# Alpha, k and q of the first six chunks: loaded four tokens per partition and turned by identity products

## The chip, the cores and the metric

The kernel runs on one NeuronCore of a Trainium2 chip. Its engines run side by side, each with its own queue of instructions that it takes in order: TensorE (PE) multiplies matrices and writes to PSUM, VectorE (DVE) and ScalarE (ACT) do element-wise work, GpSimd (POOL) does element-wise work on SBUF alone, and SyncE (SP) issues DMAs. PE loads the stationary operand of a product in a separate step, which the profile shows as PEld. The metric is the device time of one execution in microseconds (us).

## The reference

```python
# q, k, v, alpha: (4 batches, 8 heads, 768 tokens, 48), float32
for t in range(S):
    state = alpha[:, :, t, :, None] * state + np.einsum('bhd,bhe->bhde', k[:, :, t], v[:, :, t])
    y[:, :, t] = np.einsum('bhd,bhde->bhe', q[:, :, t], state)
x = y.transpose(0, 2, 1, 3).reshape(3072, 384)
h = x @ w_in                              # (384, 2048), float64
g = h * np.clip(h + 3.0, 0.0, 6.0) / 6.0
return (g @ w_out).astype(np.float32)     # (2048, 384), float64
```

A gated linear attention, which is a recurrence over the tokens, is followed by a feed-forward block with a hardswish gate. The weights go in as the bits of float64 and are turned into float32 on the chip.

## The kernel before

The recurrence is worked in chunks of 128 tokens: 24 chunks, six to a batch, in order. For each chunk the kernel loads alpha, k, q and v of all 8 heads (192 KB each), brings alpha, k and q into a layout with the head dimension on the partitions (two heads to a tile of 128 rows, 64 rows each, of which 48 are used) and the tokens on the free axis, takes the running products of alpha by two scans on DVE, scales k and q by them, and forms scores, attention and the new state on PE. Two chunks make a group of 256 tokens for the feed-forward block. Groups 0 and 1 are computed directly (`ff1`, `ff2`); from group 2 on the two products are split in the manner of fast matrix multiplication (`product1` with 20 products, `product` with 7), for which DVE adds up combinations of weights and activations.

Chunks 0 to 5 (`FIRST = 6`) come in by one way, and the later ones by another. For the first six, `load_akq` writes a ring tile with one token per partition and 8 heads of 64 places, 48 of them filled: runs of 48 numbers, 192 B each. `transposed` then turns it with four transposes on PE, one for each pair of heads, into a PSUM bank. Alpha is copied from there by ACT (`place_alpha`), k and q are read from PSUM by DVE (`scaled`). The 16 unfilled places are set once at the start, to 1 for alpha and 0 for k and q. From chunk 6 on, each partition takes four tokens, and DVE turns 32x32 blocks (`by_blocks`); no PE work is in that.

All work is issued in one order that is written out by hand as a string of steps (`run`), from which each engine gets its own instructions in that order. The steps that matter here, with a chunk as their first number:

- `la`, `lk`, `lq`, `lv`: loads of alpha, k, q, v; `w.i`: load of slice i of the weights (768 KB), all on SP's queue
- `ta`, `tk`, `tq`: turning alpha, k, q (L284; the second number is the PSUM bank); `ca`: alpha's copy on ACT (L302)
- `r`, `p`: the two scans on DVE (L311 with L315, L322); `k`, `q`: scaling (L334)
- `kb`: k back to tokens on the partitions, four transposes (L393); `ck`: its copy on ACT
- `sc`: scores (L365); `m`: mask (L375); `ya`, `yb`: attention (L478); `u`: update of the state (L452); `sm`, `st`, `sv`: the state's sums and copies (L462, L428, L438); `qa`: q for the second half of the chunk (L385); `cy`: the result to the feed-forward block (L487)
- `d1`, `d2`, `dx`, `d3`, `d4`: float64 bits of a slice to float32 (ACT L186, L196, L191, DVE L203 to L210, POOL L217)
- `fa`, `fb`, `f`: first product of groups 0 and 1 (L512, L501), `fr` and `fg` its gate (L517, L521); `b`: second product (L539)
- `x`, `y`, `xc`, `s`: sums of weights and activations on DVE; `M`, `n`, `o`: first product's pieces (L623, L629, L564 and around); `P`, `K`, `G`: second product's pieces (L726, L705, L742); `O`: store
- `z.0.n`: n products of the identity with itself into an unused bank (L555), fillers that keep PE running while it has nothing else to do

The order in which the string has them is thus the order on each queue, and a step that waits holds up what stands behind it on its engine.

Of the kernel before, what the change touches and what calls it, by code (L numbers as in the profile page):

```python
# [17 lines left out]
def kernel(  # L18
# [32 lines left out]
    nc = tc.nc  # L51
    B, H, S, D = q.shape
# [4 lines left out]
    NP = H // 2  # L57
# [3 lines left out]
    G = 2  # L61
# [11 lines left out]
    ident = consts.tile([C, C], FP, tag="ident")  # L73
# [10 lines left out]
    NR = 3  # L84
    NV = 3
    ring = {}
    rings = consts.tile([C, 3 * NR, H, 64], FP, tag="rings")
    for r in range(NR):
        for name, pad in (("a", 1.0), ("k", 0.0), ("q", 0.0)):
            t = ring[name, r] = rings[:, 3 * r + "akq".index(name)]  # L90
            (nc.vector if r == 0 else nc.gpsimd).memset(t[:, :, D:64], pad)

    vs, As = [], []
    for r in range(NV):
        t = consts.tile([C, 2, H, 64], FP, tag=f"v{r}", name=f"v{r}")
# [10 lines left out]
    for r in range(2):  # L106
        t = consts.tile([C, NP * W + 1], FP, tag=f"ax{r}")
        nc.vector.memset(t, 0.0)
        aX.append(t)
        t = consts.tile([C, NP * W], FP, tag=f"ini{r}")  # L110
# [7 lines left out]
    st, half_st, sm = (consts.tile([C, NP, D], FP, tag=name, name=name)  # L118
                       for name in ("st", "s1", "sm"))
# [115 lines left out]
    V = C // BLK  # L235
# [3 lines left out]
    for r in range(NQ):  # L239
        for name in "akq":  # L240
            quads[name, r] = consts.tile([C, NP, V, D], FP, tag=f"{name}q{r}",
                                         name=f"{name}q{r}")
# [5 lines left out]
    def pad(r):  # L248
        for name in "akq":
            for o in (BLK, 3 * BLK):  # L250
                nc.gpsimd.memset(quads[name, r][o : o + BLK, :, V - 1, D - BLK : BLK], 1.0)

    def load_akq(name, j):
        src = rows({"a": alpha, "k": k, "q": q}[name], j)
        if j < FIRST:
            nc.sync.dma_start(out=ring[name, j % NR][:, :, 0:D],
                              in_=src.rearrange("h s d -> s h d"))
            return
        to = quads[name, j % NQ]
        to = to.rearrange("r p v d -> r p (v d)")  # L260
        t = src.rearrange("(p a) (u v) d -> a u p (v d)", a=2, v=V)
        for o in range(4):
            skip = BLK * (o % 2)
            nc.sync.dma_start(out=to[BLK * o : BLK * (o + 1), :, 0 : V * D - skip],
                              in_=t[o // 2, :, :, skip : V * D])
# [10 lines left out]
    def transposed(name, j, i=None):  # L276
        if j >= FIRST:
            t = (K_t if name == "k" else Q_t)[j] = (Ks if name == "k" else Qs)[j % 2]
            by_blocks(t, name, j)
            return  # L280
        t = bank("t" + name, j, i)
        src = ring[name, j % NR]
        for p in range(NP):
            nc.tensor.transpose(  # L284
                t[:, p], src[:, 2 * p : 2 * p + 2].rearrange("s h d -> s (h d)"), ident)

    def by_blocks(to, name, j):
        nc.vector.transpose(out=to.rearrange("r p (u v) -> r p v u", v=V),
# [306 lines left out]
    for i in range(8):  # L595
        r, o = divmod(i, 3)
        spots.append(raws[r].rearrange("p n w -> p (n w)").bitcast(FP)[:, o * QB : (o + 1) * QB])
    xc = consts.tile([C, len(X_SUMS), C], FP, tag="xc")
# [68 lines left out]
    t = {1: b[0, 1], 2: spare[:, 0], 3: spare[:, 1], 4: spare[:, 2]}  # L667
# [100 lines left out]
    def run(words):  # L768
        for word in words.split():
            name, *at = word.split(".")  # L770
            steps[name](*(int(x) for x in at))

    with tc.manual_schedule():
        run("""z.0.5 z.0.3 z.0.1 qa.0.0 w.0 d2.0 d3.0 la.0 ta.0.0 z.0.8 lk.0 tk.0.1 la.1 ta.1.2
               lq.0 tq.0.3 lk.1 lv.0.0 d1.0 ca.0 r.0 p.0 k.0 kb.0.0 z.0.2 z.0.2 q.0 la.2 dx.0 ca.1
               r.1 ck.0 u.0.2.1 sm.0.0 qa.0.1 sv.0.1 tk.1.0 p.1 sc.0.2.3 w.2 lq.1 sm.0.1 k.1 m.0
               ta.2.0 z.0.2 d1.2 ca.2 d2.2 kb.1.0 ck.1 r.2 tq.1.2 q.1 dx.2 lv.1.1 u.1.3.1 z.0.3
               lq.2 w.1 lk.2 d4.0 lk.3 la.3 la.4 w.3 lq.3 lv.2.2 lk.4 w.5 pd.0 sv.0.0 pd.1 st.1
               sm.1.0 p.2 d3.2 sm.1.1 ya.0.3 yb.0 sc.1.0.2 m.1 d4.2 sv.1.1 cy.0 qa.1.1 sv.1.0 d1.1
               st.2 d2.1 dx.1 fa.0.1 tq.2.1 q.2 tk.2.3 k.2 fa.2.0 sc.2.0.2 d3.1 m.2 d4.1 ta.3.1  # L780
               ta.4.3 kb.2.0 qa.1.0 ca.3 r.3 ca.4 r.4 ya.1.2 yb.1 tk.3.1 fa.1.2 p.3 k.3 qa.2.1
               qa.2.0 cy.1 d2.3 d3.3 fb.2 fb.1 tq.3.1 q.3 sv.2.0 d1.3 ck.2 u.2.3.2 sm.2.0 d4.3
               fr.0.2.0 tk.4.0 d2.5 sv.2.1 k.4 sm.2.1 st.3 fg.0.2 d3.5 w.6 lv.3.0 lq.4 w.7 fb.0
               sc.3.1.3 m.3 kb.3.2 kb.4.0 f.0.3.3 ya.2.1 ck.3 d1.5 d4.5 d1.6 d2.6 d3.6 d4.6 sv.3.0
               qa.3.1 fr.0.1.0 fr.0.3.1 la.5 yb.2 u.3.3.2 sm.3.0 fg.0.3 fg.0.1 sm.3.1 f.0.5.0
               tq.4.3 f.0.6.3 ta.5.2 cy.2 ck.4 d2.7 qa.3.0 d1.7 d3.7 d4.7 fr.0.5.1 fr.0.0.0 sv.3.1
               fg.0.0 fg.0.5 p.4 ya.3.0 yb.3 f.0.7.2 qa.6.0 qa.12.0 qa.18.0 lq.7 w.4 d2.4 cy.3
               fr.0.6.1 w.9 d2.9 ca.5 d1.9 d1.4 dx.4 la.6 w.8 d3.4 lk.5 w.10 d3.9 ca.6 q.4 fg.0.6
               d4.9 w.12 d2.8 st.4 f.1.1.1 f.1.7.0 sc.4.0.2 f.1.3.3 qa.4.0 d1.8 fr.0.7.0 r.6 d3.8
               d4.8 d4.4 fg.0.7 m.4 fr.1.1.0 fr.1.7.1 fg.1.7 fg.1.1 d2.10 d1.10 f.1.0.2 d2.12 d3.10  # L790
               r.5 d4.10 fr.1.0.0 fr.1.3.1 fg.1.3 fg.1.0 d3.12 f.1.6.0 f.1.2.1 la.8 lq.5 lv.4.1
               w.11 w.13 lq.6 u.4.1.0 tk.5.3 sm.4.0 sv.4.0 d1.12 qa.4.1 d4.12 fa.4.3 fr.1.2.0
               fr.1.6.1 d2.11 d2.13 f.1.4.2 d1.11 sm.4.1 fg.1.2 k.5 kb.5.1 tq.5.3 d3.11 p.5 d4.11
               tq.6 fg.1.6 q.5 p.6 d3.13 d1.13 st.5 la.7 w.15 lv.5.0 lk.6 w.14 ck.5 b.0.0.1 fb.4
               ya.4.2 qa.5.1 sv.4.1 yb.4 sc.5.0.3 fr.1.4.1 cy.4 u.5.2 b.0.1 f.1.5.0 fr.0.4.0 d1.15
               sv.5.0 qa.5.0 lv.12.1 lk.7 lv.6.2 sv.12.0 sv.6.0 d4.13 xc.2.0 fg.1.4 q.6 xc.2.2
               sm.5.0 fg.0.4 ca.7 tk.6 sv.5.1 d2.15 d2.14 d1.14 d3.15 fr.1.5.1 d3.14 k.6 d4.14
               d4.15 fg.1.5 m.5 b.0.2 b.1.0.2 b.1.1 kb.6.0 ya.5.3 yb.5 b.1.2 cy.5 P.1.0.0 P.1.1.3
               lq.8 K.1.0 ck.6 u.6.2.3 b.1.3 bo.1 b.0.3 tq.7 y.5 y.1 y.3 y.0 y.6 x.0 y.9 y.7 xc.2.1
               y.11 y.13 y.2 y.8 xc.2.3 x.1 s.1.0.0 s.1.1.1 x.2 tk.7 y.10 s.1.2.3 G.1.0.0 y.4  # L800
               sm.6.0 P.1.3.3 xc.2.4 s.1.3.2 P.1.2 sc.6.2.1 y.16 y.12 y.15 s.1.4 r.7 y.17 y.19
               xc.2.5 y.20 s.1.5 xc.2.7 y.14 y.18 y.21 xc.2.6 y.23 lq.9 so.1 lv.7.0 lk.9 bo.0 K.1.2
               K.1.1 P.1.4 M.2.0.1 P.1.5 n.2.0.8 M.2.1 n.2.1.9 G.1.1.1 M.2.7.2 n.2.7.11 sv.6.1
               sm.6.1 k.7 G.1.2.2 xc.2.10 x.3 xc.2.8 p.7 q.7 st.7 y.22 xc.2.9 m.6 M.2.15.3 M.2.2
               n.2.2.10 M.2.8 kb.7.0 M.2.3 M.2.4 P.1.6 qa.7.0 ck.7 n.2.4.12 G.1.3.3 O.1.0 la.9 lk.8
               ca.9 o.2.0.0 M.2.9 u.7.1.2 ya.6.0 e.2.0.0 qa.6.1 yb.6 lv.8.2 cy.6 y.24 r.9 o.2.1.0
               M.2.10 M.2.5 n.2.10.14 e.2.1.1 n.2.5.13 sm.7.0 h.2.0 tq.8 ca.8 tk.8 h.2.1 M.2.6.0
               M.2.11 M.2.18.1 sc.7.0.3 sv.7.1 qa.7.1 n.2.11.15 n.2.18.10 sv.7.0 M.2.12 M.2.16
               M.2.19 n.2.12.12 M.2.13 sm.7.1 r.8 m.7 o.2.3.0 ya.7.3 n.2.13.12 yb.7 cy.7 M.2.14
               o.2.3.1 o.2.4.0 o.2.5.0 o.2.6.0 o.2.2.0 xc.3.1 P.2.0.1 xc.3.3 xc.3.4 e.2.3.0 xc.3.5  # L810
               o.2.2.1 e.2.2.1 M.3.0.0 M.2.17 xc.3.6 k.8 o.2.6.1 xc.3.8 h.2.3 xc.3.0 h.2.2 kt.8
               kw.8 O.1.1 st.8 K.2.0 n.3.0.12 M.3.1 P.2.1.2 e.2.6.0 h.2.6 o.2.7.0 e.2.5.1 n.3.1.9
               M.3.2 e.2.4.0 n.3.2.10 h.2.5 h.2.4 o.2.7.1 e.2.7.0 xc.3.9 xc.3.7 M.3.7.3 M.3.3
               n.3.7.13 M.3.4 M.3.8 n.3.4.8 s.2.0.14 tk.9 G.2.0.1 h.2.7 k.9 xc.3.2 kt.9 s.2.1.11
               P.2.3.2 M.3.5 o.3.0.0 M.3.9 O.1.3 lk.10 lv.9.0 la.10 s.2.4 xc.3.10 s.2.2.15 s.2.3.14
               p.8 P.2.2 o.3.1.0 s.2.5 q.8 tq.9 e.3.1.0 n.3.5.11 e.3.0.1 M.3.18.0 M.3.10 n.3.18.15
               h.3.1 p.9 M.3.19 n.3.10.14 M.3.11 K.2.1 K.2.2 P.2.5 o.3.6.0 ca.10 h.3.0 o.3.5.0
               n.3.11.8 e.3.5.0 M.3.12 n.3.12.10 q.9 O.2.0 kw.9 la.11 kr.8 kr.9 ca.11 up.8.0.1
               sp.8.2.3 M.3.13 M.3.15.0 M.3.16 G.2.2.0 o.3.3.0 sm.8.0 mp.8 o.3.4.0 sm.8.1 r.10
               sv.8.1 n.3.13.10 M.3.14 P.2.4 o.3.6.1 o.3.7.0 M.3.6.3 qa.8.0 qa.9.0 qa.8.1 sv.8.0  # L820
               st.9 e.3.4.1 lk.11 lq.11 O.1.2 la.12 lq.10 G.2.1.2 P.2.6 sm.9.0 h.3.4 sm.9.1 o.3.2.0
               ya.8.1 sv.9.1 sv.9.0 qa.9.1 st.10 G.2.3.3 yb.8 ya.9.3 yb.9 M.3.17 P.3.0.1 tk.11
               o.3.2.1 o.3.3.1 tk.10 h.3.5 O.2.2 O.2.3 la.13 lv.10.2 sv.10.0 cy.8 e.3.2.1 cy.9
               xc.4.0 xc.4.1 xc.4.3 h.3.2 xc.4.4 xc.4.5 o.3.7.1 M.4.0.0 e.3.6.0 e.3.3.1 h.3.3
# [131 lines left out]
```

## Time and profile before

| | us |
|---|---|
| median of 3 runs | 531.58 (529.79 to 532.28) |
| the profiled execution | 530.19 |
| its span, first to last instruction | 528.4 |
| PE busy | 519.6 |
| loading of PE's stationary operands (PEld) | 495.6 |
| DVE busy | 471.7 |
| ACT busy | 257.9 |
| POOL busy | 49.7 |

The profile is of one execution. Its rows give a line of the kernel, an engine, an operation, the tile written and the tile read, the shape, the count, and then busy time and mean duration, or, in a timeline, the start and the length of a run of alike instructions. A product of two float32 operands appears in the rows as more than one record of PE. Durations of PE's records overlap, since each record starts before the one ahead of it has drained; the distance between the starts is what one of them takes from the next.

### The profile page before, as it was taken

What the parts mean: (1) busy time and instruction counts of PE and PEld (TensorE: products, weight loads), DVE (VectorE), ACT (ScalarE), POOL (GpSimd) and SP (SyncE); (2) the same over time, 40 slices, a digit from 0 to 9 for tenths busy, and PEclk for the clock granted to TensorE, in tenths of its full rate; (3) what the DMA queues carried; (4) which work ended last, traced back from release to release, by engine and by line L of the source; (5) the groups of instructions that cost most, each with busy time, mean ns of one, the idle gap of its engine ahead of it and who ended that gap; (6) DMA issues with size and microseconds to landing.
All of it is one profiled execution on the core that took longest, in us unless ns stands there. A gap on an engine that the chain in (4) does not pass through costs nothing.

```text
span 528.4 us, 15020 instructions
## 1 busy us (share of the span) xinstructions
PE 519.6 (98%) x6300; PEld 495.6 (94%) x6300; DVE 471.7 (89%) x817; ACT 257.9 (49%) x503; POOL 49.7 (9%) x71
## 2 busy tenths in 40 slices
PE   7899999999999999999999999999999999999997
PEld 7788887779999999999999999999999999999997
DVE  6999999999999999999999999999999996276471
ACT  4889866013653643652544536543444545344330
POOL 6323342100000000000000100000000000000000
PEclk9999999999999999999999999999999999999999
DMA  9999987140026535355555453454163150010001
GB/s 173 222 254 265 245 242 170 29 119 1 17 58 140 131 84 120 78 110 125 123 114 133 98 117 75 111 120 118 30 139 92 30 121 13 2 31 8 9 1 45
DMA packets 124100, 54.40 MB, mean 103 GB/s; under 512 B 83328, under 2 KB 116864, under 8 KB 124032
## 3 DMA queue, kind: packets, MB, share of 16 engines
q1 hardware_dynamic: 124032, 53.44, 44.7%
q8 instruction: 49, 0.80, 0.7%
q14 instruction: 19, 0.16, 0.1%
HBM read 44.50 MB, written 8.91 MB: 101 GB/s over the span
## 4 chain that ended last, share of the span: by engine, by line
PE 81%; DVE 12%; ACT 2%; DMA 2%; issue 2%; POOL 0%; SPq 0%; DVEq 0%; ACTq 0%
PE m_ps L726 37%; PE m_ps L623 35%; PE t_ps L478 4%; PE t_ps L365 2%; PE t_ps L452 2%; DVE g_sb L521 1%; DMA rings<-in_alpha_dram 1%; DVE w L208 1%; DVE raw L210 1%; PE m_ps L555 1%; DVE w L207 1%; DVE P L322 1%; DMA qq<-in_q_dram 1%; DVE A L375 1%; PE t_ps L284 1%
## 5 line engine op out<-in xcount | busy, mean ns | idle before, releaser
L726 PE MATMUL m_ps<-w,g_sb 128*128 128x192 f32 x704 | 121.6, 326 | 0.2 <-DVE oh L742 0.2
L629 ACT COPY g_sb<-m_ps 128x512 f32<-128x512 f32 x110 | 63.5, 585 | 115.4 <-PE m_ps L623 95.1
L726 PEld LDWEIGHTS m_ps<-w,g_sb 128*128 128x128 f32 x704 | 113.8, 190 | 1.2 <-DVE oh L742 0.8
L726 PE MATMUL m_ps<-rings,g_sb 128*128 128x192 f32 x528 | 91.6, 326 | 0.8 <-DVE g_sb L670 0.8
L726 PEld LDWEIGHTS m_ps<-rings,g_sb 128*128 128x128 f32 x528 | 85.3, 190 | 1.1 <-DVE g_sb L670 1.1
L623 PE MATMUL m_ps<-xc,w 128*128 128x128 f32 x640 | 83.5, 278 | 0.0
L517 ACT ACTIVATE r<-g_sb,half 128x512 f32<-128x512 f32 x80 | 56.5, 721 | 49.1 <-DVE g_sb L564 22.8
L623 PEld LDWEIGHTS m_ps<-xc,w 128*128 128x128 f32 x640 | 77.8, 192 | 1.5 <-ACT g_sb L629 0.2
L521 DVE SCALAR_TENSOR_TENSOR g_sb<-r,g_sb 128x512 f32<-128x512 f32 x80 | 53.8, 683 | 4.6 <-ACT r L517 4.4
L623 PE MATMUL m_ps<-xT,raw 128*128 128x128 f32 x400 | 52.2, 276 | 0.0
L623 PEld LDWEIGHTS m_ps<-xT,raw 128*128 128x128 f32 x400 | 48.9, 192 | 0.2
L670 DVE TENSOR_TENSOR g_sb<-g_sb 128x512 f32<-128x512 f32 (+1 forms) x55 | 42.1, 792 | 2.6 <-PE m_ps L726 2.5
L428 POOL TENSOR_TENSOR st<-sm,R 128x192 f32<-128x192 f32 x20 | 12.1, 606 | 337.3 <-DVE sm L462 254.6
L623 PE MATMUL m_ps<-xT,w 128*128 128x128 f32 x320 | 41.7, 276 | 0.0
L623 PEld LDWEIGHTS m_ps<-xT,w 128*128 128x128 f32 x320 | 38.7, 192 | 0.2
L385 ACT COPY A<-q 48x256 f32<-48x256 f32 x88 | 35.5, 403 | 6.0 <-DVE q L334 4.7
L560 DVE TENSOR_TENSOR g_sb<-g_sb 128x512 f32<-128x512 f32 x40 | 27.0, 681 | 6.7 <-ACT g_sb L629 6.6
L501 PE MATMUL m_ps<-xT,w 128*128 128x256 f32 x144 | 32.5, 381 | 0.0
L623 PE MATMUL m_ps<-xc,raw 128*128 128x128 f32 x240 | 32.0, 276 | 0.0
L501 PEld LDWEIGHTS m_ps<-xT,w 128*128 128x128 f32 x144 | 26.9, 190 | 3.8
L311 DVE TENSOR_TENSOR_SCAN R<-t,ones 128x516 f32<-128x516 f32 x24 | 29.5, 1230 | 0.6 <-ACT t L302 0.6
L623 PEld LDWEIGHTS m_ps<-xc,raw 128*128 128x128 f32 x240 | 29.7, 192 | 0.2
(105 smaller groups left out, 722.1 us busy)
## 6 DMA issues: line engine op xcount, KB each, us to landing
raw<-in_moe_w_out_dram SPq DMA_DIRECT2D x8, 768.0 KB, 5.9
raw<-in_moe_w_in_dram SPq DMA_DIRECT2D x6, 768.0 KB, 6.3
v<-in_v_dram SPq DMA_DIRECT2D x48, 96.0 KB, 3.2
out_dram<-oh SPq DMA_DIRECT2D x44, 96.0 KB, 2.0
far<-kq SPq DMA_DIRECT2D x64, 64.0 KB, 2.2
kb<-far SPq DMA_DIRECT2D x64, 64.0 KB, 2.1
qq<-in_q_dram SPq DMA_DIRECT2D x36, 96.0 KB, 2.6
aq<-in_alpha_dram SPq DMA_DIRECT2D x36, 96.0 KB, 2.7
```

Source lines behind the costliest of these rows:

```text
L311: nc.vector.tensor_tensor_scan(out=reverse(R, n - 1, n), data0=reverse(ax, n, n), data1=reverse(ones, n, n), initial=0.0, op0=ALU.mult, op ...
L385: nc.scalar.copy(out=to[:, a], in_=Q_t[j][64 * a : 64 * a + D, :, half])
L428: nc.gpsimd.tensor_tensor(out=st, in0=sm, in1=R_t[j][:, :, 0:1].to_broadcast([C, NP, D]), op=ALU.mult)
L478: nc.tensor.matmul(y_of(j, (i + 1) // 2, p)[:, HB * b : HB * b + HB], vb[:, p, e : e + 32], A_t[j][:, b, 2 * p + a], start=(b == 0 and i = ...
L501: nc.tensor.matmul(h[:, f], w1[:, kk, o : o + C], xT_t[g][:, kk], start=(kk == 0), stop=(kk == KT - 1))
L517: nc.scalar.activation(out=to, in_=h, func=AF.Relu, bias=half, scale=1.0 / 6.0)
L521: nc.vector.scalar_tensor_tensor(out=to, in0=r, scalar=1.0, in1=h, op0=ALU.min, op1=ALU.mult)
L560: eng.tensor_tensor(out=out, in0=in0, in1=in1, op=ALU.add if s1 > 0 else ALU.subtract)
L623: nc.tensor.matmul(acc[g][i][:, f * C : (f + 1) * C], spots[w][:, f * C : (f + 1) * C], x_of(g, x), start=(first and f == 0), stop=last, s ...
L629: nc.scalar.copy(out=slots[z], in_=acc[g][i])
L670: nc.vector.tensor_tensor(out=out, in0=in0, in1=in1, op=ALU.subtract)
L726: nc.tensor.matmul(to[g], a, rhs[:, f], start=(first and f == 0), stop=(last and f == HF - 1), skip_group_check=True)
```

## The change

For chunks 0 to 5, the load puts four tokens of four head pairs on each partition, so that one run is 4 x 48 numbers, 768 B, and the even and odd heads of the pairs come by two DMAs. For chunks 0 and 1 the second of these is issued on ACT's queue, for chunks 2 to 5 on SP's. The four transposes of a tile become eight products with the identity as the moving operand: for each of the four tokens and each half of the heads, 64 places of the tile are the stationary operand, and the product goes to 64 partitions of the bank, into every fourth column. The 64 places are one token's 48 numbers and the 16 behind them; the unfilled rows of the bank hold these now. The start sets the last 128 places of each ring tile in place of the places 48 to 63 of each head. The first part of the order, 615 steps, is new. It has the same steps as before.

```diff
-            (nc.vector if r == 0 else nc.gpsimd).memset(t[:, :, D:64], pad)
+            (nc.vector if r == 0 else nc.gpsimd).memset(t[:, 6:8], pad)
...
+    TWO_QUEUES = 2
+
     def load_akq(name, j):
         src = rows({"a": alpha, "k": k, "q": q}[name], j)
         if j < FIRST:
-            nc.sync.dma_start(out=ring[name, j % NR][:, :, 0:D],
-                              in_=src.rearrange("h s d -> s h d"))
+            to = ring[name, j % NR].rearrange("r h e -> r (h e)")
+            t = src.rearrange("(p a) (u v) d -> a p u (v d)", a=2, v=V)
+            for a, queue in enumerate((nc.sync, nc.scalar if j < TWO_QUEUES else nc.sync)):
+                queue.dma_start(out=to[:, V * D * a : V * D * (a + 1)], in_=t[a])
             return
...
         t = bank("t" + name, j, i)
-        src = ring[name, j % NR]
-        for p in range(NP):
-            nc.tensor.transpose(
-                t[:, p], src[:, 2 * p : 2 * p + 2].rearrange("s h d -> s (h d)"), ident)
+        src = ring[name, j % NR].rearrange("s h e -> s (h e)")
+        for v in range(V):
+            for a in range(2):
+                o = D * (V * a + v)
+                nc.tensor.matmul(
+                    t[64 * a : 64 * a + 64].rearrange("r p (u v) -> r v p u", v=V)[:, v],
+                    src[:, o : o + 64], ident, start=True, stop=True)
...
-        run("""z.0.5 z.0.3 z.0.1 qa.0.0 w.0 d2.0 d3.0 la.0 ta.0.0 z.0.8 lk.0 tk.0.1 la.1 ta.1.2
-               lq.0 tq.0.3 lk.1 lv.0.0 d1.0 ca.0 r.0 p.0 k.0 kb.0.0 z.0.2 z.0.2 q.0 la.2 dx.0 ca.1
-               r.1 ck.0 u.0.2.1 sm.0.0 qa.0.1 sv.0.1 tk.1.0 p.1 sc.0.2.3 w.2 lq.1 sm.0.1 k.1 m.0
-               ta.2.0 z.0.2 d1.2 ca.2 d2.2 kb.1.0 ck.1 r.2 tq.1.2 q.1 dx.2 lv.1.1 u.1.3.1 z.0.3
-               lq.2 w.1 lk.2 d4.0 lk.3 la.3 la.4 w.3 lq.3 lv.2.2 lk.4 w.5 pd.0 sv.0.0 pd.1 st.1
-               sm.1.0 p.2 d3.2 sm.1.1 ya.0.3 yb.0 sc.1.0.2 m.1 d4.2 sv.1.1 cy.0 qa.1.1 sv.1.0 d1.1
-               st.2 d2.1 dx.1 fa.0.1 tq.2.1 q.2 tk.2.3 k.2 fa.2.0 sc.2.0.2 d3.1 m.2 d4.1 ta.3.1
-               ta.4.3 kb.2.0 qa.1.0 ca.3 r.3 ca.4 r.4 ya.1.2 yb.1 tk.3.1 fa.1.2 p.3 k.3 qa.2.1
...
+        run("""la.0 lk.0 la.1 lq.0 z.0.5 qa.0.0 ta.0.0 z.0.3 z.0.1 tk.0.1 ta.1.2 ca.0 lk.1 w.0
+               lv.0.0 r.0 k.0 kb.0.0 tq.0.3 lq.1 la.2 ca.1 r.1 p.0 ck.0 d2.0 d1.0 dx.0 tk.1.0 z.0.8
+               u.0.2.1 w.2 k.1 d3.0 q.0 sm.0.0 qa.0.1 p.1 ta.2.0 sc.0.2.3 z.0.2 m.0 sm.0.1 ca.2
+               sv.0.1 kb.1.0 z.0.2 z.0.2 ck.1 d2.2 d1.2 r.2 dx.2 z.0.3 tq.1.2 d4.0 la.3 lk.2 lv.1.1
+               u.1.3.1 w.1 lq.2 w.3 la.4 lk.3 w.5 lq.3 lv.2.2 st.1 sv.0.0 d3.2 sm.1.0 q.1 p.2
+               sm.1.1 ya.0.3 yb.0 sc.1.0.2 m.1 sv.1.0 cy.0 st.2 d4.2 tk.2.3 tq.2.1 fa.0.1 q.2 k.2
+               ta.3.1 sc.2.0.2 fa.2.0 qa.1.0 d1.1 d2.1 dx.1 d3.1 m.2 d4.1 pd.0 kb.2.0 ta.4.3 d2.3
+               ca.3 qa.1.1 sv.1.1 tk.3.1 ya.1.2 yb.1 fa.1.2 d3.3 r.3 k.3 d1.3 ck.2 ca.4 cy.1
...
```

## The prediction, made before the changed kernel was built or run

> **What bounds the kernel now.** I read the chain of waits first, then the busy time by stretch, then TensorE's (PE's) groups by shape in the stretches that the change touches, and last the timeline of PE for what one record costs. The page's summary of the chain:
>
> ```profile
> PE 81%; DVE 12%; ACT 2%; DMA 2%; issue 2%; POOL 0%; SPq 0%; DVEq 0%; ACTq 0%
> ```
>
> PE ends the run. The busy time by stretch (PE, PEld, DVE, ACT, POOL, clock, DMA share, GB/s):
>
> ```profile
> 0.00:10.30 10.30, 7.66 (x35) 7.39 (x36) 6.43 (x15) 5.31 (x5) 6.45 (x19) 1.00 1.06 173
> 10.30:20.00 9.70, 7.95 (x146) 6.80 (x145) 9.25 (x16) 6.13 (x12) 5.28 (x15) 1.00 1.28 234
> ...
> 30.00:110.90 80.90, 80.51 (x876) 64.90 (x865) 78.77 (x123) 51.69 (x89) 23.75 (x18) 1.00 0.76 187
> ```
>
> From 30 to 110.9 us both PE and VectorE (DVE) are almost full, and the chain goes through DVE there. A busy PE can still have room, so I counted its demand: the records of each shape times the pace at which such records follow one another. First the counts from 30 to 110.9 us:
>
> ```profile
> L501 PE MATMUL m_ps<-xT,w 128*128 128x256 f32 x144 | 32.5, 381 | 0.0
> L539 PE MATMUL m_ps<-w,g_sb 128*128 128x384 f32 x64 | 21.8, 491 | 0.0
> L512 PE MATMUL m_ps<-xT,w 128*128 128x128 f32 x72 | 8.7, 275 | 0.0
> ...
> L478 PE MATMUL t_ps<-A,v 128*32 128x64 f32 x280 | 4.9, 220 | 0.2 <-DVE A L375 0.2
> L284 PE MATMUL t_ps<-ident,rings 128*128 128x128 f32 x28 | 4.4, 278 | 0.0
> ```
>
> Then the paces, from the timeline:
>
> ```profile
> 3.76 1.91 PE L555 MATMUL m_ps<-ident 128*128 128x128 f32 x8
> 6.85 1.09 PE L284 MATMUL t_ps<-ident,rings 128*128 128x128 f32 x4 [1.18 <-DMA rings<-in_alpha_dram]
> 10.80 1.47 PE L284 MATMUL t_ps<-ident,rings 128*128 128x128 f32 x12
> 14.23 0.66 PE L284 MATMUL t_ps<-ident,rings 128*128 128x128 f32 x4
> 14.81 0.69 PE L365 MATMUL t_ps<-q,k 48*64 48x64 f32 x32
> 20.83 1.10 PE L478 MATMUL t_ps<-A,v 128*32 128x64 f32 x64
> 59.60 10.63 PE L501 MATMUL m_ps<-xT,w 128*128 128x256 f32 x48
> ```
>
> A row's length less its last record's own time, over the other records, is the pace. Twelve transposes: (1.47 - 0.27) / 11 = 0.109 us. 256 moving columns: (10.63 - 0.38) / 47 = 0.218, or 0.85 ns a column. By 0.109 for 128 columns, 0.162 for 192, 0.218 for 256, 0.322 for 384 and 0.013 to 0.015 for the small tiles, PE's records of 30 to 110.9 us need 77 us of 80.9. That is 95%, with 4 us of room in some thirty small gaps. The same count for 0 to 30 us gives 18.4 of 30. The rest is 1.5 us before the identity is there, 1.2 of waiting for the first alpha, about 3.6 of a slow PE (the fillers at 3.76 run at 0.213, the transposes at 6.85 no faster, those at 10.80 at 0.109, while the granted clock reads 1.00 throughout) and some 5 of waits for DVE and ACT. So PE has about 11 us of room in the first 30 us, 4 until 110.9, and next to none after.
>
> **The turn, the largest term.** A tile (alpha, k or q of one chunk) is turned now by four transposes, one record each: 4 x 0.109 = 0.44 us. The new code makes eight products with the identity. The fillers show what a product is: 26 calls of one are 52 records at L555, so two each. That makes 16 records of 128 moving columns, each filling one half of the array's columns. Side by side in pairs they cost 16 x 0.109 / 2 = 0.87 us; one after the other 1.74. The nearest rows are the small tiles: L478 uses a quarter of the columns, (1.10 - 0.22) / 63 = 0.014 us, four of them 0.056, just what 64 columns take at 0.85 ns; L365 the same. They run fully side by side, so I take 0.87, that is +0.43 a tile and +7.8 us for 18 tiles, and keep 1.74 (+23 us) as the far end. Below 0.87 is excluded, since no row streams faster than its columns.
>
> The step between full-width and narrow records: from the last transpose of the row at 14.23 to the scores at 14.81 is 0.25 us where 0.109 would do, so 0.14 lost, and 0.05 in the other direction (u at 70.16, transposes at 70.67). Turns that stood among full-width records gain two such steps; between 0 and 36 steps, I take 0.8 us, with 0 and 3 as the ends. The Trainium skill (TensorEngine Tiling, Key Properties and Restrictions and Gotchas) says that column tiling excludes the fp32 transpose mode and that a change of tiling mode drains the engine. It speaks against this change, and no row here shows a drain as long as a product's own 0.22 us. By that length the sum would rise by up to 8 us instead of 0.8.
>
> **The loads.** A tile comes now as 1024 runs of 192 B; 6 to 10 us, when nothing else moves, reads 163 GB/s, so 1.2 us a tile. It becomes 256 runs of 768 B. The nearest rows are the quads' loads of that size (96 KB, 2.6 us to landing, rings 5.5 to 6.6) and mixed stretches at 224 to 257 GB/s, so about 0.8 us a tile. That frees some 7 us of transfer, but PE waits for a DMA once only, 1.2 us at 6.85. The first alpha now leaves at 1.24 behind 768 KB of weights and lands at 6.72; put first, at 0.74, it lands at 3.4 (the rows' 2.6) to 5.2 (the weights, first now, took 4.8 to their reader, of which 2.7 is their size at 290 GB/s), I take 4.0. The ACT queue issues six halves at 0.44 to 0.58 us, 3 us in a stretch where ACT is busy 5.3 of 10.3. They and the table load (1.28) end before the first copy at 6; without that cover they would put up to 1.1 us ahead of the second copy (`ca.1`). For chunks 2 to 5 SP issues two halves instead of one; SP is off the chain. The memsets keep their size. `w.0` goes behind five loads (about 4 us later); its first reader on DVE, `d3.0`, is now sixth there, at 13.9. `pd` and `lv.12`/`sv.12` with their POOL memsets (0.33 and 0.5 us) and SP issues move later, past nothing that PE waits for; `lk.6` to `lk.11`, the `lq` beside them, `O.1.0` and `st.8` shift by a few places.
>
> **The opening, by its new order.** Five fillers from 1.47 at 0.213 end at 3.7. `ta.0` at 4.0, PE still slow: 1.7 us, readable at 5.95; copy (0.59) to 6.6; `r.0` (1.4) to 8.0. Fillers to 7.4, `tk.0` to 8.9 with PE fast from about 8.3, `k.0` 9.1 to 9.7. `ta.1` to 9.8, `ca.1` to 10.65, `r.1` to 12.1. Then DVE runs through: `p.0` 13.3, `k.1` 13.9, `d3.0` 15.2, `q.0` 15.8, seven steps of 6.9 us, `q.1` done at 22.7. The scores of chunk 1 start at 22.8; now it is 21.86. Behind them stand `tk.2`, `tq.2`, `fa.0`, `ta.3`, `sc.2`, `fa.2`, `kb.2`, `ta.4`, 7.6 us with the scores, so 30.5 where the same steps now end at 29.1: **+1.4**. DVE's first scan is 2 us earlier, but it loses 2.1 us to waits for turns. When PE gets fast matters: now a first run without a gap of 4.2 us (1.47 to 5.68) did not do it, and a second one did after 3.4 (6.85 to 10.3). If PE is fast at 5 to 7, the opening ends at +0.2; at 10.3, at +2.3. The Trainium skill (TensorE: Matmul & The Clock Gate, Part 1) has a free-running window of 3.4 us that must be busy as a whole, which these two runs agree with; by it a gap ahead of `ta.0` decides between the two ends.
>
> Seven turns are left after that (`k`, `q` of 3 and 4, all of 5): 7 x 0.43 = 3.0, with the steps 3.5. The gaps from 30 to 126 us are waits of 0.1 us or so at hand-overs; I let a third of 4.2 be filled, -1.4: **+2.1**. DVE has 2 us of room there (78.77 of 80.90) and the same work, so nothing comes back from it. After the new order ends the steps are the old ones on a full PE. Sum +3.5 us on the profiled execution's 530.19 = 533.7. The median is 1.39 above that execution, so 535.0 in its terms.
>
> **The rivals.** (A) Absorbed, 0.28: the turns fill the waits of the first 30 us and most of the small gaps. For it: 11 us of room stands against 4.7 us in the first eleven turns. Against: the room is made of waits on DVE, which the new order does not end. It gives -0.5 to +2, 531 to 533.5. (B) Faster, 0.09: the chain names DVE from 30 to 110.9. If DVE is what counts and a turn costs PE no more than about 0.5 us, the earlier alpha (1.2 of PE's waiting) and half of the 5 us of waits go: -3.5, 528. Also for it: 2.3 us of DVE work (`k.6`, `p.6`, `q.6` and the like) moved behind `G.1.0.0`. Against: a PE demand of 95% plus 3 us. (C) Much slower, 0.13: half-width products do not pair, or each step to them drains the array; the outputs, written to every fourth column, have no row like them either. At 1.74 a turn +23 less 5 absorbed, 549; with drains alone 542. It decides from 1.1 us a turn on. (D) The two queues do nothing: ACT's halves wait behind its table load, 1.3 us on the first alpha, within the 5.2 above.
>
> **How the numbers follow.** The forecast has 0.50 (533 to 539, the opening's +0.2 to +2.3 and the steps' 0 to 3 about it). 0.5% is 2.7 us, about what a measurement of this kernel can tell from no change. Slower by more: 0.43 of the forecast's 0.50, 0.02 of A, all of C: 0.58. Within: 0.07 + 0.26 = 0.33. Faster: 0.09. The range 530.5 to 541 takes the forecast and nearly all of A.
>
> **What would show it.** L284's records go from 72 to 288, 128x64, at 0.056 us each in a row of 16. The first turn starts near 4.0, the second scores near 22.8; PE's small gaps from 30 to 126 us shrink below 4; `G.1.0.0` on DVE comes at 112 to 115 (now 110.49). I am wrong if a turn takes 0.5 us or 1.5, or if the stretch to 30 us ends earlier than now.

## The result, and the profile after

The changed kernel takes 555.5 us (554.11 to 558.09, four runs) against 530.88 (529.79 to 532.28) for the kernel before beside it: a ratio of 1.0468, 95% interval 1.042 to 1.0516. Slower was forecast, but by 3.5 us and not by some 25, and the range ended at 541. The profiled execution took 558.09 us with a span of 556.3. The chain of waits of the changed kernel sums to

```profile
PE 73%; DMA 11%; DVE 8%; SPq 5%; ACT 2%; issue 1%; DVEq 0%; ACTq 0%
```

PE had 81% before and DMA 2. That chain in order of time shows where the transfers have come in:

```profile
0.74 3.79 DMA rings<-in_alpha_dram
4.55 9.32 DMA rings<-in_k_dram
13.89 6.58 DMA rings<-in_k_dram
20.52 1.97 PE t_ps L290 x14
...
53.37 9.16 DMA qq<-in_q_dram
62.55 9.36 DMA rings<-in_alpha_dram
72.00 9.48 DMA raw<-in_moe_w_out_dram
```

Of the first 20.5 us, 19.7 are three DMAs, one after the other: ACT's half of alpha of chunk 0, SP's half of k of chunk 1 and ACT's half of that k. By the instructions in the trace they use one completion semaphore, and each is issued when the one before has landed. There are three more of over 9 us from 53 on. The busy time by stretch (columns as in the prediction):

```profile
0.00:10.30 10.30, 7.13 (x42) 6.29 (x44) 4.42 (x12) 1.87 (x2) 6.44 (x19) 1.00 0.40 122
10.30:20.00 9.70, 4.60 (x50) 3.34 (x46) 3.22 (x4) 3.41 (x5) 0.00 (x0) 0.88 0.56 158
20.00:30.00 10.00, 9.48 (x132) 8.74 (x132) 6.57 (x12) 4.56 (x8) 2.18 (x2) 0.78 0.54 146
30.00:110.90 80.90, 73.89 (x978) 62.38 (x977) 65.56 (x105) 59.25 (x96) 29.09 (x32) 0.98 0.77 202
```

From 10.3 to 20 us PE has 50 records where it had 146, and DVE 3.2 us of work where it had 9.25. The DMA engines, 1.28 by this count before, are at 0.56: the transfers are what is waited for, and yet the engines stand half idle. The granted clock falls to 0.88 and 0.78 behind the gaps. The DMA view of the first 20 us, in 40 slices, shows why. First the kernel before, then the one after (tenths of 16 engines, then what they moved):

```profile
DMA  0005669999999999999999999999999999999999
GB/s 0 0 0 53 66 152 369 418 379 292 253 187 163 163 163 163 165 161 163 164 163 157 169 163 168 201 217 373 385 353 283 217 172 164 185 162 192 220 347 357
```

```profile
DMA  0000111222222279999585822222222323889998
GB/s 0 0 0 0 31 34 55 81 86 92 92 92 92 94 208 305 354 349 283 157 204 135 203 81 89 93 94 94 106 94 74 69 93 104 178 200 338 381 299 225
```

Runs of 192 B took 163 GB/s from all sixteen engines. Runs of 768 B move 92 to 94, with a busy share of 2 tenths, that is 4 of 16 engines. So one tile of 192 KB takes 2.1 us at best and not 0.8. (The stretches at 300 and more are slices of the weights.)

The turn itself and the waits of ACT, from the timeline after:

```profile
5.67 1.97 PE L290 MATMUL t_ps<-ident,rings 128*64 128x128 f32 x16 [1.70 <-DMA rings<-in_alpha_dram]
13.89 0.54 ACTq L261 DMA_DIRECT2D rings<-in_k_dram  x1
16.56 0.58 ACT L309 COPY t<-t_ps 128x512 f32<-128x512 f32 x1 [8.26 <-DMA raw<-in_moe_w_in_dram]
33.77 0.69 PE L372 MATMUL t_ps<-q,k 48*64 48x64 f32 x32
34.45 1.97 PE L290 MATMUL t_ps<-ident,rings 128*64 128x128 f32 x32
```

Two turns in a row on a fast PE are 32 records in 1.97 us: (1.97 - 0.27) / 31 = 0.055 each, so 0.88 a turn, where 0.87 was forecast. The second copy of alpha comes at 16.56, and ACT waited 8.26 us for it; the second scores start at 33.77, where 22.8 was forecast and 21.86 stood before.

### The profile page after: what moved, and what is told of

It is laid out like the page before. It is cut to its first block, busy times and chain, and to the rows that moved or that the text cites. A ratio compares the mean times of both kernels' runs of the same rounds, so it can differ in the third digit from the quotient of the medians.

```text
span 556.3 us, 15472 instructions
## 1 busy us (share of the span) xinstructions
PE 535.2 (96%) x6516; PEld 507.0 (91%) x6516; DVE 471.8 (85%) x817; ACT 257.9 (46%) x503; POOL 52.3 (9%) x71
## 4 chain that ended last, share of the span: by engine, by line
PE 73%; DMA 11%; DVE 8%; SPq 5%; ACT 2%; issue 1%; DVEq 0%; ACTq 0%
PE m_ps L733 32%; PE m_ps L630 28%; PE m_ps L546 4%; PE t_ps L485 4%; DMA rings<-in_k_dram 3%; DMA raw<-in_moe_w_out_dram 3%; DMA rings<-in_alpha_dram 2%; PE t_ps L372 2%; DMA qq<-in_q_dram 2%; PE t_ps L459 1%; PE t_ps L290 1%; DVE g_sb L567 1%; DVE g_sb L528 1%; SPq L278 1%; SPq L268 1%
```

## The experiments

All ratios are to the kernel before on the same chip, with 95% intervals, three or five rounds each. "The spread load" below is this edit, in which the load's outermost dimension has 32 tokens instead of the 4 pairs of heads, with the same runs of 768 B and the columns of the products changed to match:

```diff
-            t = src.rearrange("(p a) (u v) d -> a p u (v d)", a=2, v=V)
+            t = src.rearrange("(p a) (u v) d -> a u p (v d)", a=2, v=V)
...
-                    t[64 * a : 64 * a + 64].rearrange("r p (u v) -> r v p u", v=V)[:, v],
+                    t[64 * a : 64 * a + 64].rearrange("r p (u v) -> r v u p", v=V)[:, v],
```

**The spread load in the changed kernel.**

> The changed kernel with the tokens ahead of the head pairs in the load (a u p instead of a p u) and the product's output columns permuted to match; sizes, counts and order stay. Theory of the few engines: the changed kernel moves about 120 runs of 768 B a microsecond at 36 ns each, which is what four DMA engines can do, because the slowest dimension of the source is the four head pairs; with 32 tokens there, all 16 engines take part, a tile's half lands in about 2.5 us instead of 4 to 9, and some 20 us come back: 533 to 538, what is left over the kernel before being PE's products. Theory of the second queue: the halves on ACT's queue still wait for earlier transfers, 550 or more. Theory of the products: they are the whole loss, so no change, 553 to 557.

540.85 against 529.43, ratio 1.0206 (1.0166 to 1.0247). Some 14 us of the loss are gone with the order of two dimensions. The DMA view of its first 20 us:

```profile
DMA  0000496999796799999999999998665641997699
GB/s 0 0 0 0 111 300 157 260 278 274 232 134 119 243 389 385 385 277 209 170 230 303 328 378 380 387 353 258 179 194 164 137 78 33 190 112 111 262 418 391
```

The plateau at 92 is gone and the engines are full. The same bytes in the same runs: what was lost is the number of engines that one DMA was dealt out to. The records of the transfers agree: in the changed kernel each 768 B took 36 ns and 120 of them went by per us, 4.3 at a time, and a half tile ended with 4 signals, while the other DMAs of this kernel end with 16. The Trainium skill (DMA: Bandwidth & Descriptors, Why a DMA increments its semaphore by 16 and not by 1) says that a DMA goes to the largest number of engines up to 16 that divides the outermost dimension of both sides; with 4 pairs against 128 partitions that is 4, and the trace agrees.

**The products alone in the kernel before**, with its loads and order.

```diff
-            nc.tensor.transpose(
-                t[:, p], src[:, 2 * p : 2 * p + 2].rearrange("s h d -> s (h d)"), ident)
+            for a in range(2):
+                nc.tensor.matmul(t[64 * a : 64 * a + 64, p], src[:, 2 * p + a], ident,
+                                 start=True, stop=True)
```

> The kernel before, its loads and its order, with each transpose of a tile replaced by two products with the identity (16 records of half width for 4 records). If the products add to PE's demand as forecast (0.43 us a tile, 18 tiles) and are partly absorbed: +3 to +8 us, 534 to 539. If they are the whole loss: 550 or more. If PE has room for them: within 2 us of before.

543.42 against 529.43, ratio 1.0263 (1.0223 to 1.0303), so 14 us, between the two expectations. PE's records at the paces of the prediction make 8.2 us more. Of the rest, 3.2 us are one halt in the middle of a row of scores:

```profile
22.82 0.46 PE L366 MATMUL t_ps<-q,k 48*64 48x64 f32 x14
26.48 0.53 PE L366 MATMUL t_ps<-q,k 48*64 48x64 f32 x18 [3.21 <-issue]
```

Behind it PE is slow for a while: its next twelve records of the first product take 2.93 us, at full pace 1.60. Nothing in the profile releases the halt. A packet of instructions was moving at that time (16 KB, from 23.2 us), but the kernel before has one at 22.9 without a halt, and no run tests it. So this run does not give the price of the products alone.

**One queue, in the changed kernel as it is:** `TWO_QUEUES = 0`, all loads on SP.

> The changed kernel with all its loads on SP's queue. Theory of the second queue: the first copies on ACT stood behind a half that waited until 13.9 us, so 5 us or more come back: below 551. Theory of the few engines: the four engines are as slow as before, and the time stays within 3 us of the changed kernel's 555.5.

556.2, ratio 1.0509 (1.0475 to 1.0542), against 1.0468 with two: as long as four engines carry a load, the second queue is not the loss.

**The new order alone in the kernel before.**

> The kernel before with the new order alone (its loads of 192 B runs and its transposes). If the new order is good for any load that comes soon enough, within 2 us of before, 529 to 533; with the slower 192 B loads ahead of the weights it may lose 1 to 4. If the order itself is the loss: 540 or more.

534.49, ratio 1.0103 (1.0063 to 1.0142). The new order with the old loads costs 5 us, between its second and its third expectation. It leans on loads that come sooner: PE waits 1.45 us for an alpha ahead of 15.15 us and 1.79 us for a v ahead of 21.27.

**The spread load, all on SP, with the old order and with the new.**

> The changed kernel with 16 engines to a load, all loads on SP's queue, and the order of the kernel before. Products on 18 tiles stay. Theory that the products' 8 us of PE are not absorbed and the order is worth little: 537 to 540, close to the kernel with 16 engines and the new order (540.9). Theory that the new order costs 5 us also with these loads: 533 to 537. Theory that the new order pays once the loads are fast: above 542.

> The changed kernel with 16 engines to a load, new order, all loads on SP's queue. In the run with two queues ACT's half of k of chunk 1 left only when the transfer that used its semaphore before had landed (7.56 us), and ACT's next copies stood behind it. If that wait sits on the path, 2 to 4 us come back: 537 to 539. If the second queue is neither good nor bad: within 1.5 us of 540.9.

539.33, ratio 1.0171 (1.0144 to 1.0198), and 538.56, ratio 1.0161 (1.013 to 1.0192): with these loads the two orders are 0.5 us apart, which these intervals cannot tell from 2 us either way. The second is 2.4 us below the first experiment, with intervals that overlap, so the second queue was measured again further down.

**Products for chunks 3 to 5 alone in the kernel before** (nine tiles, turned from 27 us on, the products of the second experiment under `if j >= 3`).

> The kernel before with products in place of transposes for chunks 3 to 5 alone (9 tiles, 9 x 0.45 = 4.0 us of PE's time, all of it after 25 us, where PE has next to no gaps). If nothing of it is absorbed: +3.5 to +4.5, so 533 to 534. If a third of it fits into the small gaps, as forecast: +2 to +3. If products cost more than PE's time (14 us for 18 tiles): +6 to +8.

536.44 against 530.35, ratio 1.0115 (1.0087 to 1.0144): 6.1 us, or 0.68 a tile, where 0.43 is PE's own work. That lies at the low end of the third expectation.

```profile
30.00:110.90 80.90, 80.85 (x985) 66.03 (x974) 74.21 (x116) 51.34 (x87) 23.76 (x18) 1.00 0.77 185
```

DVE does 74.21 us of work from 30 to 110.9 instead of 78.77: it is held up by PE and not the other way round. None of the added time was absorbed. Some 1.4 us are steps between full-width and half-width records, read from the distances of their starts: 0.093 us lost going to half width and 0.147 coming back, so 0.24 for a group of turns among full-width records and 0.15 for one beside small tiles, in eight groups. The remaining 0.8 was not traced.

**Alpha of chunk 0 loaded first in the kernel before** (`la.0` moved to the head of the order).

> The kernel before with one step moved: the load of alpha of chunk 0 goes ahead of the fillers and of the first slice of weights. Its 192 KB land about 2 to 3 us sooner, PE's wait of 1.2 us at 6.85 goes, the weights land 1.2 us later. If the opening is a chain from the first alpha: -1 to -2.5 us. If the chain runs over the weights or over DVE's conversions, or PE gets to its full pace later for it: -0.5 to +1.

530.28 against 530.35, ratio 1.0000 (0.9982 to 1.0017).

```profile
5.47 1.06 PE L284 MATMUL t_ps<-ident,rings 128*128 128x128 f32 x4
...
10.05 0.63 PE L284 MATMUL t_ps<-ident,rings 128*128 128x128 f32 x4 [0.58 <-DVE t L315]
12.03 0.63 PE L393 MATMUL t_ps<-ident,k 128*128 128x128 f32 x4 [1.34 <-DVE k L334]
```

The first turn starts at 5.47 instead of 6.85, and PE then stands still 1.9 us at 10 and 12 for DVE. DVE's first scan of alpha starts at 8.59 us in both kernels: the copy of alpha stands on ACT behind two conversions of weights, whose load now comes 0.8 us later (5.52 before, 6.32 here). So in the order of before PE's one wait for a DMA was worth nothing; what an earlier alpha is worth in an order without the weights ahead of it, this run does not say.

**Which halves on ACT's queue**, all three with the spread load: none, those of chunk 0, those of chunks 0 and 1 (`TWO_QUEUES` 0, 1, 2).

> The same with all loads on SP, as the reference of the other two: 8 us above the kernel before.

> The changed kernel with the loads on sixteen engines, and only chunk 0's three halves on ACT's queue (SP issues those of chunk 1). Theory: what the second queue costs is the wait of ACT's half of k of chunk 1, with ACT's queue and the first copy of alpha behind it; without that half the loss goes and this is level with the kernel that has all loads on SP, about 2.4 us below the one with chunks 0 and 1 on ACT. Rival 1: the time goes by ACT's three issues at the start themselves (1.9 us ahead of its table load): then it lies at the two-queue kernel's time. Rival 2: the queues make no difference and the 2.3 us between the two earlier runs were the measurement: all three within 1 us.

> The same with chunks 0 and 1 on ACT's queue (the kernel of the first experiment again, in five rounds beside the other two): theory and rival 1 about 2.4 us over the one-queue kernel; rival 2 within 1 us of it.

| halves on ACT | median us (before 530.5) | ratio |
|---|---|---|
| none | 539.18 | 1.0152 (1.0127 to 1.0177) |
| chunk 0 | 535.9 | 1.0118 (1.0086 to 1.0151) |
| chunks 0 and 1 | 542.3 | 1.0218 (1.0193 to 1.0243) |

Chunk 1's three halves on ACT's queue cost 1.0218 - 1.0118 = 1%, 5.3 us, and their intervals are far apart. Chunk 0's give perhaps 2 us, not resolved. With none on ACT, SP takes about 0.65 us to issue each half, and the chain of the first 30 us runs over these issues, from 0.75 to 10.66 us almost without a break, to a load of alpha of chunk 2 that PE turns at 16.07. The 5.3 us are not the issues as such. ACT's rows with chunks 0 and 1 on it:

```profile
7.79 0.56 ACTq L261 DMA_DIRECT2D rings<-in_k_dram  x1
11.51 0.54 ACTq L261 DMA_DIRECT2D rings<-in_q_dram  x1
12.15 0.58 ACT L309 COPY t<-t_ps 128x512 f32<-128x512 f32 x1 [5.71 <-DMA rings<-in_k_dram]
```

and with chunk 0 alone:

```profile
8.98 0.59 ACT L309 COPY t<-t_ps 128x512 f32<-128x512 f32 x1 [2.44 <-PE t_ps L290]
```

The two issues at 7.79 and 11.51 stood in ACT's queue ahead of the copy of alpha 1 and let it run at 12.15 instead of 8.98. The instructions in the trace say what they waited for: the first ten microseconds' DMAs of both queues use eight semaphores in turn, and each waits first for the DMA that had the semaphore before it. ACT's half of k of chunk 1 shares one with SP's half, issued at 3.66, and ACT's half of q with a 768 KB slice of the weights, issued at 4.34. So ACT, and its copies behind it, waited for SP's transfers. ACT's half of k came late by the same wait, and this ends last in the chain of that kernel:

```profile
3.66 4.12 DMA rings<-in_k_dram
...
7.79 6.20 DMA rings<-in_k_dram
...
14.04 1.97 PE t_ps L290 x14
```

The half landed at 14.0 us. With chunk 0 alone on ACT, SP's two halves of that k landed at 7.3 and 7.7, and PE had turned it by 11.4, here by 15.9. PE stood still for 2.8 us ahead of it and was slow afterwards, with a granted clock of 0.65 from 10.3 to 20 us against 1.00. No run parts the late half from the late copies.

**A mixture that the runs pointed to:** the kernel with chunk 0 on ACT, but the new loads and products for chunks 0 and 1 alone.

```diff
+        if NEW <= j < FIRST:
+            nc.sync.dma_start(out=ring[name, j % NR][:, :, 0:D],
+                              in_=src.rearrange("h s d -> s h d"))
+            return
...
+        if j >= NEW:
...
+                nc.tensor.transpose(
+                    t[:, p], src[:, 2 * p : 2 * p + 2].rearrange("s h d -> s (h d)"), ident)
```

> The kernel with chunk 0's second halves on ACT's queue and sixteen engines, but with the new loads and the products for chunks 0 and 1 alone; chunks 2 to 5 are loaded and turned as in the kernel before. Theory: what was left of the loss there (6.3 us) is PE time of turns that stand in a full stretch, 0.68 us a tile by the run with products for chunks 3 to 5; 12 tiles less give 8 us back, of which some goes where the old loads bind in the opening: about 1 to 2 us below the kernel before, 528.5 to 530. Rival: the rest of the loss comes from the order or from the loads' place in the queue; then it stays near 534 to 536, or goes up, since chunk 2's tiles come by the slower loads.

538.1 against 529.62, ratio 1.016 (1.0137 to 1.0184). My theory missed: no time came back. PE's rows:

```profile
20.86 0.57 PE L470 MATMUL t_ps<-v,kb 64*48 64x48 f32 x30 [0.69 <-DMA v<-in_v_dram]
22.68 1.11 PE L496 MATMUL t_ps<-A,v 128*32 128x64 f32 x64 [1.25 <-DVE s L480]
...
25.50 1.97 PE L294 MATMUL t_ps<-ident,rings 128*128 128x128 f32 x8
27.27 2.76 PE L530 MATMUL m_ps<-xT,w 128*128 128x128 f32 x12
```

PE's work fell by 5.5 us against the kernel with all six chunks new, but with the old loads of chunk 2 and later the new order makes PE wait, and it then runs slowly for some 5 us: eight transposes in 1.97 us (at full pace 1.04), twelve records of L530 in 2.76 (at full pace 1.60), with a granted clock of 0.68 from 20 to 30 us. Loads, order and turns hang together; the order for this mixture was not made. No kernel tried is faster than the one before.

## Why the prediction was wrong

**Where the 25 us are.** By ratios of 530.5 us:

| step | ratio | us |
|---|---|---|
| four engines instead of sixteen a load | 1.0468 to 1.0218 | 13.3 |
| halves of chunk 1 on ACT's queue | 1.0218 to 1.0118 | 5.3 |
| the rest: products, new order, spread loads | 1.0118 | 6.3 |

The first has a wide interval (10 to 16), and it was taken off first; with four engines the queues make no difference that shows (third experiment), so the two do not simply add. The third step was not taken apart in the changed order.

**The loads: the step that failed.** "so about 0.8 us a tile" came from the quads' rows, as the nearest of 768 B. They have the same run, but 32 tokens outermost, and go to 16 engines; the new load has 4 head pairs outermost and goes to 4. The size of a run was the same, the dimension that decides was not looked at. From this came "That frees some 7 us of transfer", where 92 GB/s against 163 makes each tile 0.9 us longer, and every load behind it in SP's queue later. ACT's half of the first alpha landed at 4.5 and SP's at 5.6, and the first turn, which needs both, started at 5.67 (forecast 4.0, at most 5.2). The halves of the second k came at 13.9 (SP's) and 20.5 (ACT's).

With sixteen engines the 0.8 us come out only where two queues issue. From 2.5 to 5.5 us the kernel with chunks 0 and 1 on both queues moves 242 GB/s, 0.8 us a tile, with a busy share of the engines of 0.86. The one with all loads on SP moves 152, 1.3 us a tile, with a share of 0.55: two issues of 0.65 us are what a tile takes there, and that is no faster than the 163 GB/s of before. "SP is off the chain" failed with it.

**The second queue, rival D, failed too.** It was given "1.3 us on the first alpha", for halves that wait behind ACT's table load; the trace has the table load behind the first four halves, at 4.07. The price lay in chunk 1's halves, which the sum passed over as 3 us of issues beside a busy ACT: 5.3 us with the spread load, for a wait inside ACT's queue that makes the half of k late, with alpha's copy behind it. The prediction named what is queued behind the second copy, but gave it 1.1 us.

**The rest of the sum came near, in part by luck.** The kernel with the spread load and only chunk 0 on ACT comes closest to what the prediction described: loads that come quickly, no wait in ACT's queue. It takes 535.9 (535.3 to 540.4), where 535.0 was forecast, but it was singled out of three after its time was known. Its rows of PE:

```profile
3.90 1.98 PE L290 MATMUL t_ps<-ident,rings 128*64 128x128 f32 x16
...
22.06 0.78 PE L372 MATMUL t_ps<-q,k 48*64 48x64 f32 x32
...
29.82 1.97 PE L290 MATMUL t_ps<-ident,rings 128*64 128x128 f32 x32
```

First turn 3.90 (forecast 4.0; the halves of alpha land at 3.2 and 3.5, and the fillers ahead of the turn end then), second scores 22.06 (22.8), `ta.4`, the first half of the last row, done at 29.82 + 0.87 = 30.7 (30.5); DVE reaches `G.1.0.0` at 112.6 (112 to 115). So the opening cost +1.6 (forecast +1.4), and two errors cancel in it. PE is at its full pace from 6.1 us on, for which the prediction had +0.2, and the second scores are 0.7 early. The steps from them to `ta.4` then take 8.6 us and not 7.6: the 7.6 are the records at their paces alone, with nothing for the hand-overs between them, and they were set against 7.2 us of before (21.86 to 29.1) that have the hand-overs in them and turns that are 1.7 us shorter. By the paces of the prediction, PE's records make 8.2 us more than before over the whole run, and the time that they leave in the first 30 us falls from 11.7 to 8.1.

**After the opening one term was wrong.** The profiled execution of that kernel is 5.4 us above that of before, so 3.8 came after the opening where 2.1 was forecast. Seven turns at 0.43 make 3.0, as forecast; the time that PE's records leave behind 30 us grew from 18.0 us in all to 18.5, where steps of 0.5 and a filling of 1.4 were to take 0.9 from it. "I let a third of 4.2 be filled" failed: nothing was, and the run with nine late tiles shows it by itself (+6.1 for 3.9 us of work). The steps are 0.093 us into half width and 0.147 back, where 0.14 and 0.05 had been read from the rows. The Trainium skill (TensorEngine Tiling, Key Properties) says that a change of tiling mode drains the engine; the losses here stay below the 0.22 us that the prediction set for a drain, and no run shows whether they are that drain.

**The rivals.** A (absorbed): the opening did absorb 3.1 of 4.7 us, near the 3.3 that the forecast itself had, and the rest absorbed nothing. B (faster by the earlier alpha, if DVE is what counts): with nine late tiles the time went up with PE's work and DVE fell behind, so from 30 to 110.9 us it is not DVE; the earlier alpha alone was worth 0.0 us in the order of before (interval -1.0 to 0.9). C had the nearest time, 549, by a mechanism that is not there: products pair at 0.055 to 0.056 a record.

## What to carry to other kernels

When a load is laid out anew, compare the outermost dimension of both sides, and not only the length of a run: here the order of two dimensions decided between 4 and 16 engines and 13 us. Before a DMA is put on the queue of an engine that also computes, look for what it may have to wait for there and what stands behind it; a low busy share of the DMA engines beside a chain full of DMAs is the row that gives too few engines, or too slow an issue, away. An order written for one set of loads can cost time with another (5 us here with the old ones), so a change of loads, turns and order at once is taken apart by undoing one at a time.

## What the runs showed of the hardware

- A DMA whose outermost dimension is 4 ran on four engines, at 92 to 94 GB/s with runs of 768 B; with 32 outermost, the same runs went by at 242 GB/s when SP and ACT issued them and at 152 when SP alone did, at about 0.65 us an issue of 96 KB.
- In these kernels the DMAs of SP and ACT share eight completion semaphores in turn, so that one engine's issue can wait for the other's transfer: with chunks 0 and 1 on ACT, its half of q waited 3.2 us (from the end of the issue ahead of it, 8.35, to 11.51) for a slice of the weights that SP had issued at 4.34.
- A wait of 1 to 2 us on PE may be followed by some 5 us at about half the pace, as in the mixture (eight transposes in 1.97 us against 1.04), and in another run it is not (1.17 us at 21 us, with chunk 0 on ACT, at a clock of 1.00 throughout). What decides was not tried.
- A change from full-width to half-width records (128x64) costs PE 0.091 to 0.096 us, and 0.147 the other way; from small tiles to half-width records it is 0.12 to 0.14.
- PE halted once for 3.2 us with nothing in the profile that releases it, in the kernel with products alone. The cause stays open.
